# Feed-forward tiles in groups of eight and six, a written plan of shares, and single homes for three buffers

## The chip, the cores and the metric

The kernel runs on one core of a Trainium2 chip. The core has five engines with queues of their own: TensorE (PE in the profile; its weight loads are listed as PEld), VectorE (DVE), ScalarE (ACT), GpSimd (POOL) and SyncE (SP), which here does nothing but start transfers. They work at the same time and wait for each other by semaphores. The metric is the time of one execution on the device in microseconds; the kernel before takes 1460.91 us (median of three runs, 1458.57 to 1462.61).

## The reference

One transformer-like block over 2048 tokens of width 512, all in float32:

```python
xn = layernorm(x)
q, k, v = split(xn @ wqkv)                 # 32 heads of 16
o = softmax(q @ k.T * 16 ** -0.5) @ v      # per head, over all 2048 keys
s = o @ wo
f = (silu(xn @ w_gate) * (xn @ w_up)) @ w_down   # inner width 1792
out = x + s * silu(f)
```

## The kernel before

**Products.** Where float32 accuracy is wanted at the fast matmul form, an operand is split into a rounded part and a rest (`hi`, `lo`), and a product is three: hi·hi, lo·hi, hi·lo. In this text a *product* is one call of `both` (L169 to L171): two matmuls with 64 rows each, one into the bank `bankx` and one into `banky`, which run side by side on PE. The two banks are added by VectorE when a tile is done, and PE can begin the next tile only when both have been read.

**Stages.** The first part (to L749) normalises, turns and projects the tokens to q, k and v, which go to DRAM. Then comes attention, where 88% of the time lies: 32 units (8 groups of 4 heads × 4 blocks of 512 queries), each of 8 steps, together 256 steps (L773 to L812). In a step PE computes the scores of two key tiles of 128 keys, ScalarE takes their exponentials (four of 128×1024 each, L787), and PE multiplies the step before's exponentials with the values (`values`, L358). The scores lie in two buffers in PSUM, so the second key tile's scores wait for the first one's exponentials, and so on from step to step. PE's order in a step: two pairs of score matmuls, the values of the step before, two pairs of score matmuls, and then a *share* of other work.

**The work dealt out.** That other work is a queue of generators (L400 to L403): the feed-forward network for the four blocks of 512 tokens (`ffn`, L180), then the output projection (`project_out`, L317), which for the last block goes over three quarters of the features and for the other three blocks over all. Each `yield` is one product, and `fill(n)` draws n of them. `share` (L423) decides how many a step gets: it divides a tile into equal parts so that the size of a part is near the pace (what is left over the steps that are left). A tile of 24 products so gives 8, 8, 8; one of 21 gives 11 and 10, or 7, 7, 7; one of 12 gives 12, or 6 and 6. In all 2160 products are dealt out over the 256 steps, and 12 are kept for the end.

**Feed-forward.** For each block of tokens the 14 tiles of 128 inner features are taken in two groups of seven (`FG`). First each tile's gate and up product (24 products, `fx` is the block's normalised tokens, `gu` the split weights); at its end ScalarE takes a tanh (`th`, L198), VectorE makes the gated tile `ga` (L199, L200) and splits it into `hh`, and splits the raw w_down rows `wdr` into `wd` (`split_hidden`, L160; L141, L142). Then four output tiles of 128 tokens, each over the group's seven tiles, 21 products; after the first group they are stored in `facc`, after the second added to it as `y` (L218 to L223), and `store_gate` (L173, another tanh in `th`) stores their gate. These calls stand in a list `after` and are made in the next step (`catch_up`). With the last tile of the second group `load_fx` (L144) fetches the next block's `fx`.

**Loads.** All of SyncE's transfers are issued in the order in which the program writes them; one that has to wait for its buffer holds up those behind it. `load_wd(i + 1)` (L186) stands at the start of tile i, with two homes for `wdr`, ahead of `load_gu(i + 2)`. A unit's queries (`load_q`, L803) are fetched one unit ahead, in its first step.

**Output projection.** Each tile of 128 tokens is 12 products (9 for the last block's part). VectorE adds the banks into `y` (L336, L337), GpSimd multiplies by the gate and adds the input (`store_out`, L312) and stores. `ready` counts a block's split inputs, and `fill` stops at a block that isn't ready. In the last unit `load_gate` and `gate_rest` (L344, L352) prepare the last block's rows with eight operations on VectorE (L354, L355). After the last step come the last tile, the last values, and the last block's last quarter (L813 to L853).

Of the kernel before, what the change touches and what calls it, by code (L numbers as in the profile page):

```python
# [9 lines left out]
F32 = mybir.dt.float32  # L10
# [9 lines left out]
P = 128  # L20
S = 2048
D = 512
# [7 lines left out]
KT = S // P  # L30
NG = H // 4
NF = F // P
FG = NF // 2
VW = 4 * (DH + 1)
NROW = 3 * DH + 2
HALF = 64
# [1 line left out]
RING = NB + 1  # L38
DC = D // HALF
LIMIT = 160.0  # L40
EPS = 1e-5
QSLOT = (0, 1, 0)
KSLOT = (0, 0, 1)
# [3 lines left out]
def tile_block(ctx: ExitStack, tc: tile.TileContext, x, wqkv, wo, w_gate, w_up, w_down, out):  # L47
# [84 lines left out]
        gu[i] = (hi, lo)  # L132

    def load_wd(i):
        raw = two.tile([P, D], F32, tag="wdr", name="wdr")
        sp.dma_start(raw, w_down[(i % NF) * P:(i % NF + 1) * P])
        wdr[i] = raw

    def split_wd(i):
        f = i % FG  # L140
        dve.tensor_copy(wd[:, f, 0], wdr[i])  # L141
        dve.tensor_sub(wd[:, f, 1], wdr[i], wd[:, f, 0].bitcast(F32))  # L142

# [16 lines left out]
    def split_hidden():  # L160
        while kept:
            f, i, ga = kept.pop(0)
            dve.tensor_copy(hh[:, f, 0], ga)
            dve.tensor_sub(hh[:, f, 1], ga, hh[:, f, 0].bitcast(F32))
            split_wd(i)

    halves = [slice(h * HALF, (h + 1) * HALF) for h in range(2)]

# [2 lines left out]
            mm(bank, lhs[h], rhs[h], start=start, stop=stop)  # L171

    def store_gate(y, r):  # L173
        th = two.tile([P, D], F32, tag="th", name="th")
        act(th, y, AF.Tanh, scale=0.5)
        dve.scalar_tensor_tensor(y, th, 1.0, y, op0=ALU.add, op1=ALU.mult)
        pool.dma_start(g_d[r:r + P], y)


    def ffn(b):  # L180
        for grp in range(2):
            for f in range(FG):
                i = b * NF + grp * FG + f
                if i + 1 < NB * NF:
                    split_gu(i + 1)
                    load_wd(i + 1)  # L186
                if i + 2 < NB * NF:
                    load_gu(i + 2)
                hi, lo = gu.pop(i)
                n = 0  # L190
                for c in range(DC):
                    for wt, j in ((hi, 0), (hi, 1), (lo, 0)):
                        both(wt[:, c], fx[:, j, c], n == 0, n == 3 * DC - 1)
                        n += 1
                        if n == 3 * DC:
# [8 lines left out]
                            if grp == 1 and f == FG - 1 and b + 1 < NB:  # L204
                                load_fx(b + 1, 0)
                                load_fx(b + 1, 1)
                            elif grp == 1 and f == FG - 1:
                                load_wo(0)
                                load_wo(1)
                        yield 3 * DC - n  # L210
            for t in range(NT):
                n = 0
                for f in range(FG):
                    for a, w in ((0, 0), (0, 1), (1, 0)):
                        both(hh[:, f, a, t * P:(t + 1) * P], wd[:, f, w], n == 0, n == 3 * FG - 1)
                        n += 1
                        if n == 3 * FG and grp == 0:
                            dve.tensor_copy(facc[:, t], bankx)  # L218
                            dve.tensor_add(facc[:, t], banky, facc[:, t])
                        elif n == 3 * FG:  # L220
# [6 lines left out]
                        yield 3 * FG - n  # L227


    wor = {}  # L230

    def load_wo(c):
        wor[c] = two.tile([P, D], F32, tag="wdr", name="wor")
        sp.dma_start(wor[c], wo[c * P:(c + 1) * P])

    def split_wo(c):
# [80 lines left out]
    def project_out(b, n=DT):  # L317
        catch_up()
        for j in range(NT):
            t = b * NT + j  # L320
            i = 0
            for c in range(n):
                for a, w in ((0, 0), (0, 1), (1, 0)):
                    lo, hi = lhs[b, c][a][:, j * P:(j + 1) * P], fx[:, w, c]
                    if t == end:
                        mm(bankx, lo, hi, start=i == 0, stop=i == 3 * n - 1)  # L326
                    else:
                        both(lo, hi, i == 0, i == 3 * n - 1)
                    i += 1
                    if i == 3 * n and n == DT:  # L330
                        y = two.tile([P, D], F32, tag="th", name="y")
                        if t == end:
                            after.append(partial(act, y, bankx, AF.Copy, scale=0.5))
                            after.append(partial(store_out, t, y))
                        else:
                            dve.tensor_scalar(y, bankx, 0.5, None, op0=ALU.mult)  # L336
                            dve.scalar_tensor_tensor(y, banky, 0.5, y, op0=ALU.mult, op1=ALU.add)  # L337
                            store_out(t, y)
                    elif i == 3 * n:
                        dve.tensor_copy(facc[:, j], bankx)  # L340
                        dve.tensor_add(facc[:, j], banky, facc[:, j])
                    yield 3 * n - i

    def load_gate():  # L344
        for i in range(2):
            last.extend((two.tile([P, D], F32, tag="wdr", name="last"), on[i]))
        for t in range(NT):
            r = rows[(NB - 1) * NT + t]
            sp.dma_start(gate[t], g_d[r])
# [47 lines left out]
    u0 = units - NB + 1  # L397


    queue = [[None, ffn(b), NF * 3 * DC + 2 * NT * 3 * FG] for b in range(NB)]  # L400
# [5 lines left out]

    now = -1

    left = 0

    def fill(n):
        nonlocal given, left
        while n > 0 and queue and (queue[0][0] is None or ready[queue[0][0]] == DT):
            left = next(queue[0][1])
            queue[0][2] -= 1
            if not queue[0][2]:
                queue.pop(0)
# [2 lines left out]

    def share():  # L423
        pace = max(1.0, (total - rest - given) / (units * steps - now))
        if left:
            n = left
        elif queue and queue[0][0] is None and len(queue) > NB:
            n = 3 * (DC if ffn_tiles() else FG)
        else:
            n = 3 * DT if queue and queue[0][0] is not None else 3 * (DT - 1)  # L430
        n = -(-n // max(1, round(n / pace)))
        fill(min(n, total - rest - given))


    def ffn_tiles():
        return given % (NF * 3 * (DC + NT)) % (FG * 3 * (DC + NT)) < FG * 3 * DC


    with ExitStack() as pro:
# [89 lines left out]
                dve.tensor_scalar(rt, n1, rt, None, op0=ALU.mult)  # L529

        def norm(t):
            xn[t] = two.tile([P, D], F32, tag="th", name="xn")
            dve.tensor_scalar(xn[t], xin[:, t], mv[:, t, 0:1], rs[:, t:t + 1], op0=ALU.subtract, op1=ALU.mult)  # L533

        def turn_x(b, t, between=None):
# [230 lines left out]

    now = 0
    split_hidden()
    prev = None

    exps = []
    settled = mybir.DependencyInfo(mybir.DependencyClass.Sync, mybir.DependencyReason.DATA)
    for u in range(units):  # L773
        g, b = divmod(u, NB)
        q = qst[u % 2]
        for kp in range(steps):
            now = u * steps + kp
            probs = []
            for i in range(2):
# [9 lines left out]
                        tc.add_manual_dep(exps[-1].ins, exps[-3].ins.name, settled, reason="order of the slots' writes")  # L789
                    probs.append(pr)  # L790
                if now == i == 0:
                    fill(5)
                if i == 0:
                    catch_up()
                if i == 0 and prev:
# [38 lines left out]
    def gated(t):  # L834
        dve.scalar_tensor_tensor(y[t], outs[t], 0.5, gate[t], op0=ALU.mult, op1=ALU.mult)  # L835
# [42 lines left out]
```

## Time and profile before

| | |
|---|---|
| runs | 1460.91 us median, 1458.57 to 1462.61 |
| the profiled execution | 1459.36 us, of which the span from the first to the last instruction is 1457.6 |
| granted clock of PE | 0.998 |
| PE busy | 1441.6 us, 99% of the span |
| ScalarE busy | 1094.5 us, 75%; 992.5 of it the 1024 exponentials, 1023 ns each |
| VectorE, GpSimd busy | 537.7 us (37%), 88.2 us (6%) |
| attention steps | from 168.16 us on; the last begins at 1436.31 |

The first numbers of a timeline line are the start and the length in us, then engine, line, operation, output and inputs; a bracket at the end is how long the engine had stood idle and for whom. Neighbouring instructions of one kind are merged to one line (x4). A line of the stretches view gives the stretch, its length, each engine's busy time, the granted clock, and last the busy share of the DMA engines and GB/s. Matmuls are pipelined and their ends are modelled, so PE is shown busy while it waits inside a merged line; starts tell more than busy time.

### The profile page before, as it was taken

How to read it: one execution, taken by the hardware profiler on the slowest of the kernel's cores; microseconds unless marked ns; L12 is line 12 of the kernel's file. 1: busy time of each engine (PE TensorE's matmuls, PEld its weight loads, DVE VectorE, ACT ScalarE, POOL GpSimd, SP SyncE). 2: the span in 40 equal slices, each digit the busy share in tenths (PEclk: the TensorE clock that was granted, in tenths of full speed). 3: DMA queues.
4: the chain of work that ended last, by engine and by line, in shares of the span. 5: the costliest groups of instructions: out<-in, count | busy, mean ns of one | idle time of the engine just before them, and what ended most of it. 6: DMA issues, size and time to landing. Idle time of an engine off the chain costs nothing.

```text
span 1457.6 us, 26766 instructions
## 1 busy us (share of the span) xinstructions
PE 1441.6 (99%) x11237; PEld 806.6 (55%) x11237; DVE 537.7 (37%) x905; ACT 1094.5 (75%) x1219; POOL 88.2 (6%) x105
## 2 busy tenths in 40 slices
PE   9999999999999999999999999999999999999997
PEld 7777655555555555555555555555555555555544
DVE  6543343124333432234233422343243314334535
ACT  4433588788878887888788878887888778887774
POOL 4100200000000000000000000000000000000234
PEclk9999999999999999999999999999999999999999
DMA  8889652033273331143715311437135202423252
GB/s 267 272 284 287 168 121 58 15 86 88 67 172 84 92 78 34 39 110 72 171 36 120 87 24 34 105 86 171 56 76 130 56 12 46 105 63 128 91 188 73
DMA packets 129556, 154.92 MB, mean 106 GB/s; under 512 B 12700, under 2 KB 79260, under 8 KB 128404
## 3 DMA queue, kind: packets, MB, share of 16 engines
q1 hardware_dynamic: 123940, 130.38, 36.0%
q0 software_dynamic: 5200, 22.22, 4.0%
q8 instruction: 91, 1.49, 0.4%
q10 hardware_dynamic: 288, 0.52, 0.1%
q14 instruction: 37, 0.30, 0.1%
HBM read 111.13 MB, written 41.94 MB: 105 GB/s over the span
## 4 chain that ended last, share of the span: by engine, by line
PE 95%; ACT 2%; DVE 1%; DMA 1%; issue 0%; DVEq 0%; ACTq 0%
PE acc L364 32%; PE bankx L171 29%; PE score L785 20%; PE ps L561 6%; PE banky L171 4%; PE ps L563 3%; ACT pr L787 1%; DMA q_d<-parts 1%; PE acc L538 0%; DVE facc L354 0%; PE bankx L326 0%; DMA facc<-in_A_x_dram 0%; DVE y L835 0%; DVE xn L533 0%; DVE y L838 0%
## 5 line engine op out<-in xcount | busy, mean ns | idle before, releaser
L787 ACT ACTIVATE pr<-score 128x1024 f32<-128x1024 f32 x1024 | 992.5, 1023 | 237.7 <-PE score L785 235.0
L364 PE MATMUL acc<-pr,vst 128*17 128x512 f32 x4096 | 489.2, 595 | 0.0
L785 PE MATMUL score<-qst,kst 50*128 50x512 f32 x2048 | 360.1, 424 | 2.9 <-ACT pr L787 2.0
L785 PEld LDWEIGHTS score<-qst,kst 50*128 50x128 f32 x2048 | 177.8, 184 | 273.2 <-ACT pr L787 236.7
L171 PE MATMUL bankx<-fx,guh 64*128 64x512 f32 x896 | 288.4, 392 | 0.0
L171 PE MATMUL banky<-fx,guh 64*128 64x512 f32 x896 | 288.3, 391 | 0.0
L364 PEld LDWEIGHTS acc<-pr,vst 128*17 128x17 f32 x4096 | 93.9, 96 | 235.4 <-issue 234.6
L199 DVE SCALAR_TENSOR_TENSOR ga<-th,bankx 128x512 f32<-128x512 f32 x56 | 38.5, 687 | 464.1 <-ACT th L198 464.1
L171 PEld LDWEIGHTS bankx<-fx,guh 64*128 64x128 f32 x896 | 165.8, 185 | 32.7 <-issue 0.4
L171 PE MATMUL bankx<-fx,gul 64*128 64x512 f32 x448 | 175.4, 391 | 0.0
L171 PE MATMUL banky<-fx,gul 64*128 64x512 f32 x448 | 175.3, 391 | 0.0
L171 PEld LDWEIGHTS banky<-fx,guh 64*128 64x128 f32 x896 | 165.7, 185 | 4.1
L171 PE MATMUL bankx<-wd,hh 64*128 64x512 f32 x672 | 165.8, 389 | 0.0
L171 PE MATMUL banky<-wd,hh 64*128 64x512 f32 x672 | 165.7, 388 | 0.0
L171 PEld LDWEIGHTS bankx<-wd,hh 64*128 64x128 f32 x672 | 124.0, 184 | 24.9
L171 PEld LDWEIGHTS banky<-wd,hh 64*128 64x128 f32 x672 | 124.0, 184 | 2.1
L171 PEld LDWEIGHTS bankx<-fx,gul 64*128 64x128 f32 x448 | 82.8, 185 | 17.5
L171 PEld LDWEIGHTS banky<-fx,gul 64*128 64x128 f32 x448 | 82.8, 185 | 1.8
L561 PE MATMUL ps<-xt,wh 128*128 128x512 f32 x256 | 80.9, 397 | 0.0
L131 DVE TENSOR_TENSOR gul<-gur,guh 128x1024 fp32r<-128x1024 f32 x56 | 68.6, 1226 | 2.1
L218 DVE COPY facc<-bankx 128x512 f32<-128x512 f32 x16 | 11.1, 691 | 131.1 <-PE banky L171 103.9
L600 ACT CAST parts<-ps 128x512 fp32r<-128x512 f32 x32 | 18.7, 585 | 52.0 <-PE ps L561 24.4
(146 smaller groups left out, 1042.7 us busy)
## 6 DMA issues: line engine op xcount, KB each, us to landing
fx<-xt_d SPq DMA_DIRECT2D x32, 512.0 KB
gur<-in_B_w_gate_dram SPq DMA_DIRECT2D x56, 256.0 KB
gur<-in_B_w_up_dram SPq DMA_DIRECT2D x56, 256.0 KB
wdr<-in_B_w_down_dram SPq DMA_DIRECT2D x56, 256.0 KB
kst<-k_d SPq DMA_DIRECT2D x192, 64.0 KB
qst<-q_d SPq DMA_DIRECT2D x192, 64.0 KB
xt_d<-xt POOLq DMA_DIRECT2D x8, 1024.0 KB, 8.0
q_d<-parts SPq DMA_DIRECT2D x16, 512.0 KB
```

Of the source, the lines that this page charges most:

```text
L131: dve.tensor_sub(lo, raw, hi.bitcast(F32))
L171: mm(bank, lhs[h], rhs[h], start=start, stop=stop)
L199: dve.scalar_tensor_tensor(ga, th, 1.0, bankx, op0=ALU.add, op1=ALU.mult)
L218: dve.tensor_copy(facc[:, t], bankx)
L364: mm(a[h * 32:h * 32 + DH + 1], v[:, kt % CT, h * (DH + 1):(h + 1) * (DH + 1)], probs[2 * i + h // 2][:, h % 2], start=kt == 0, stop=kt == ...
L561: mm(ps, w, a[:, c], start=n == 0, stop=n == 3 * DT - 1)
L563: mm(ps, a[:, c, tokens], w, start=n == 0, stop=n == 3 * DT - 1)
L600: nc.scalar.copy(parts[:, 0], ps)
L785: mm(score[j][:, h], k[r, j, kc * P:(kc + 1) * P], q[r, j], start=True, stop=True)
L787: exps.append(act(pr, score[j], AF.Exp, scale=0.25))
```

## The change

The 14 tiles of a block are taken as eight and six. An output tile of a group has 24 or 18 products for 21; their sum over a block is the same. `share` no longer works out its part: `plan` writes all 256 shares in a list before the first step. Gate tiles go as 8, 8, 8, tiles of the six-group as 9, 9, those of the eight-group as 8, 8, 8 or as 12, 12 (two parts for nine of 16, spread evenly by `HALVED`), the last block's projection as one share of 9 a tile, and the other projection tiles by `OUT_PARTS` as 12 or as 6, 6. Tile 1, of which 15 and 9 products were drawn in two steps, now has three steps of 8, five of them drawn early in step 0 as before.

`hh` and `wd` have eight places each for seven. Room for them comes from buffers that had two homes and have one: `wdr` (w_down rows, and the rows of `wo` and one row of `x` later), `th` (both tanhs, and the projection's `y`), and the pool `late` of the normalisation. `load_wd` is issued in a tile's first third for the tile itself, no longer a tile ahead; `load_wo` one quarter ahead and not two. The normalised tokens of the first part move to the tag `ga`, the last block's third row of `x` goes to `on[2]`, and the tail's rows lie in homes of the exponentials.

```diff
-FG = NF // 2
+GROUPS = (slice(0, 8), slice(8, NF))
+FG = 8
...
+FIRST = 5
+HALVED = 9
+OUT_PARTS = (2, 2, 1, 1, 1, 1, 1, 2, 1, 2, 2)
...
     def load_wd(i):
-        raw = two.tile([P, D], F32, tag="wdr", name="wdr")
+        raw = one.tile([P, D], F32, tag="wdr", name="wdr")
...
     def store_gate(y, r):
-        th = two.tile([P, D], F32, tag="th", name="th")
+        th = one.tile([P, D], F32, tag="th", name="th")
...
-        for grp in range(2):
-            for f in range(FG):
-                i = b * NF + grp * FG + f
+        for grp, part in enumerate(GROUPS):
+            nf = part.stop - part.start
+            for f in range(nf):
+                i = b * NF + part.start + f
                 if i + 1 < NB * NF:
                     split_gu(i + 1)
-                    load_wd(i + 1)
...
                         n += 1
+                        if n == DC and i:
+                            load_wd(i)
                         if n == 3 * DC:
-                            th = two.tile([P, TB], F32, tag="th", name="th")
+                            th = one.tile([P, TB], F32, tag="th", name="th")
...
     def next_out(t):
         split_wo(t)
-        if t + 2 < DT:
-            load_wo(t + 2)
+        if t + 1 < DT:
+            load_wo(t + 1)
...
-                        y = two.tile([P, D], F32, tag="th", name="y")
+                        y = one.tile([P, D], F32, tag="th", name="y")
...
     def load_gate():
-        for i in range(2):
-            last.extend((two.tile([P, D], F32, tag="wdr", name="last"), on[i]))
+        last.extend(on[:3] + [one.tile([P, D], F32, tag="wdr", name="last")])
...
+    shares = []
+
+    def plan():
+        def tile_of(n, parts):
+            shares.extend([n // parts] * parts)
+
+        halved = 0
+        for i in range(2 * NB):
+            nf = GROUPS[i % 2].stop - GROUPS[i % 2].start
+            for _ in range(nf - (i == 0)):
+                tile_of(3 * DC, 3)
+            for t in range(NT):
+                if nf == FG:
+                    halved += HALVED
+                    tile_of(3 * nf, 3 - halved // (NB * NT))
+                    halved %= NB * NT
+                else:
+                    tile_of(3 * nf, 2)
+        for _ in range(NT):
+            tile_of(3 * (DT - 1), 1)
+        for parts in OUT_PARTS:
+            tile_of(3 * DT, parts)
+        shares[0] -= FIRST
+
+    def blocked():
+        return not queue or queue[0][0] is not None and ready[queue[0][0]] < DT
+
     def share():
-        pace = max(1.0, (total - rest - given) / (units * steps - now))
...
-        fill(min(n, total - rest - given))
+        if not blocked() and shares:
+            fill(shares.pop(0))
...
         def norm(t):
-            xn[t] = two.tile([P, D], F32, tag="th", name="xn")
+            xn[t] = two.tile([P, D], F32, tag="ga", name="xn")
...
-    late = ctx.enter_context(tc.tile_pool(name="late", bufs=2))
+    late = ctx.enter_context(tc.tile_pool(name="late", bufs=1))
...
+    spare, *y = [ppool.tile([P, 2, TB], F32, tag="pr", name="y") for _ in range(3)]
+    y = [i[:, n] for i in y for n in range(2)]
     turned = []
     for n in range(2):
         normalise(units - 1, n * half, (n + 1) * half, partial(low, 0) if n else None)
-        turned.append(late.tile([P, TB], F32, tag="o2", name="o2"))
+        turned.append(spare[:, n])
...
-    y = [where.tile([P, D], F32, tag=tag, name="y") for where, tag in ((two, "ga"), (late, "o1")) * 2]
```

More of the change, by code (lines that the diff above doesn't have):

```diff
@@ L203, in ffn @@
                                 split_hidden()
-                            if grp == 1 and f == FG - 1 and b + 1 < NB:
+                            if grp == 1 and f == nf - 1 and b + 1 < NB:
                                 load_fx(b + 1, 0)
                                 load_fx(b + 1, 1)
-                            elif grp == 1 and f == FG - 1:
+                            elif grp == 1 and f == nf - 1:
                                 load_wo(0)
-                                load_wo(1)
                         yield 3 * DC - n
@@ L212, in ffn @@
                 n = 0
-                for f in range(FG):
+                for f in range(nf):
                     for a, w in ((0, 0), (0, 1), (1, 0)):
-                        both(hh[:, f, a, t * P:(t + 1) * P], wd[:, f, w], n == 0, n == 3 * FG - 1)
+                        both(hh[:, f, a, t * P:(t + 1) * P], wd[:, f, w], n == 0, n == 3 * nf - 1)
                         n += 1
-                        if n == 3 * FG and grp == 0:
+                        if n == 3 * nf and grp == 0:
                             dve.tensor_copy(facc[:, t], bankx)
                             dve.tensor_add(facc[:, t], banky, facc[:, t])
-                        elif n == 3 * FG:
+                        elif n == 3 * nf:
                             y = two.tile([P, D], F32, tag="ga", name="y")
@@ L226, in ffn @@
                                 after.append(partial(next_out, t))
-                        yield 3 * FG - n
+                        yield 3 * nf - n
     wor = {}
     def load_wo(c):
-        wor[c] = two.tile([P, D], F32, tag="wdr", name="wor")
+        wor[c] = one.tile([P, D], F32, tag="wdr", name="wor")
         sp.dma_start(wor[c], wo[c * P:(c + 1) * P])
@@ L397, in tile_block @@
     u0 = units - NB + 1
-    queue = [[None, ffn(b), NF * 3 * DC + 2 * NT * 3 * FG] for b in range(NB)]
+    queue = [[None, ffn(b), NF * 3 * (DC + NT)] for b in range(NB)]
     queue += [[None, project_out(NB - 1, DT - 1), NT * 3 * (DT - 1)]]
@@ L407, in tile_block @@
     now = -1
-    left = 0
     def fill(n):
-        nonlocal given, left
-        while n > 0 and queue and (queue[0][0] is None or ready[queue[0][0]] == DT):
-            left = next(queue[0][1])
+        nonlocal given
+        while n > 0 and not blocked():
+            next(queue[0][1])
             queue[0][2] -= 1
@@ L419, in fill @@
             given += 1
-    def share():
-        pace = max(1.0, (total - rest - given) / (units * steps - now))
[L425 to L431, printed above, removed]
-        fill(min(n, total - rest - given))
-    def ffn_tiles():
-        return given % (NF * 3 * (DC + NT)) % (FG * 3 * (DC + NT)) < FG * 3 * DC
+    shares = []
[21 more added lines that the diff above has]
+        return not queue or queue[0][0] is not None and ready[queue[0][0]] < DT
+    def share():
+        if not blocked() and shares:
+            fill(shares.pop(0))
     with ExitStack() as pro:
@@ L768, in tile_block @@
     split_hidden()
+    plan()
     prev = None
@@ L791, in tile_block @@
                 if now == i == 0:
-                    fill(5)
+                    fill(FIRST)
                 if i == 0:
```

5 lines of the change are left out of this document (2 added, 3 removed).

## The prediction

> **What bounds the kernel now.** First the chain that ended last, on the profile's page (share of the span by engine, then by line):
>
> ```profile
> PE 95%; ACT 2%; DVE 1%; DMA 1%; issue 0%; DVEq 0%; ACTq 0%
> PE acc L364 32%; PE bankx L171 29%; PE score L785 20%; PE ps L561 6%; PE banky L171 4%; PE ps L563 3%; ACT pr L787 1%; DMA q_d<-parts 1%; PE acc L538 0%; DVE facc L354 0%; PE bankx L326 0%; DMA facc<-in_A_x_dram 0%; DVE y L835 0%; DVE xn L533 0%; DVE y L838 0%
> ```
>
> TensorE (PE) carries it, and the number of its instructions is the same after the change. So the only question is where PE stands waiting inside the 256 attention steps. The chain doesn't show that; the waits do (engine, line, waited for: us in total, times, longest):
>
> ```profile
> PEld score L785 <- ACT pr L787: 236.7, 317, 0.9
> SPq L136 <- DVE wd L142: 427.9, 45, 35.8
> ```
>
> A score weight load waits for ScalarE's exponentials 317 times. Mostly other matmuls run meanwhile, so I looked at how long steps are. In the timeline of PE every step starts with the four score matmuls of its first key tile (start us, length, what), so the difference of two such starts is a step. First the end of a group of feed-forward tiles, then the output projection:
>
> ```profile
> 421.40 0.63 PE L785 MATMUL score<-qst,kst 50*128 50x512 f32 x4
> 426.89 0.63 PE L785 MATMUL score<-qst,kst 50*128 50x512 f32 x4
> 432.15 0.65 PE L785 MATMUL score<-qst,kst 50*128 50x512 f32 x4
> 436.74 0.87 PE L785 MATMUL score<-qst,kst 50*128 50x512 f32 x4
> 441.55 0.86 PE L785 MATMUL score<-qst,kst 50*128 50x512 f32 x4
> 446.36 0.86 PE L785 MATMUL score<-qst,kst 50*128 50x512 f32 x4
> ```
> ```profile
> 1358.84 0.62 PE L785 MATMUL score<-qst,kst 50*128 50x512 f32 x4
> 1364.59 0.64 PE L785 MATMUL score<-qst,kst 50*128 50x512 f32 x4
> 1368.97 0.39 PE L785 MATMUL score<-qst,kst 50*128 50x512 f32 x2
> 1369.54 0.50 PE L785 MATMUL score<-qst,kst 50*128 50x512 f32 x2 [0.18 <-ACT pr L787]
> 1373.77 0.39 PE L785 MATMUL score<-qst,kst 50*128 50x512 f32 x2
> ```
>
> The six rows of the first list bound steps of 11, 10, 7, 7 and 7 products: 5.49, 5.26, 4.59, 4.81, 4.81. The next, of 8, takes 5.06, although an 8 in a row of eights takes 4.84. A product in a run is 0.2325 us, so a 7 should take 4.61 each time. The first does; then the score group is longer (0.87 for 0.65), because its second half waits for ScalarE. So ScalarE sets a floor of 4.80 a step, and what a short step can't pay is paid by the next. The second list bounds 12, 6 and 6 (the third and fourth row are one group that the wait splits): 5.75, 4.38, 4.80, then 12 again at 6.20. A six loses 4.80 − 4.37 = 0.43, a seven 0.2, and steps from eight up are paid at 4.84 (8), 5.07 (9), 5.26 (10), 5.50 (11), 5.75 (12).
>
> **The change, part by part.** All sums are against the profiled execution, 1459.36 us, which is 1.55 below the median of 1460.91.
>
> *Shares, feed-forward output tiles.* Before, each of eight groups takes 399.82 to 446.36 = 46.54 us for its nine output steps (11, 10 three times, 7, 7, 7), and 0.22 in the next eight: 46.76, times 8 = 374.1. After, from the plan: the four groups of six give 32 nines; in the four groups of eight, 9 of 16 tiles go as two twelves (18) and 7 as three eights (21). 32 × 5.07 + 18 × 5.74 + 21 × 4.84 = 162.2 + 103.3 + 101.6 = 367.1, and some 0.05 for the tanh in the first step of each group (in the 46.54 it is in the first 11, 5.56 for 5.50): 367.5. A twelve is 5.73 (11 plus a product) to 5.75 (the row). That is −6.6, in 71 steps for 72.
>
> *The step given back.* Tile 1 now takes 8, 8, 8 in steps 0 to 2, where it took 15 and 9 in two (168.16 to 178.65, 10.5 us). Step 0 has no value matmuls to cover the exponentials, which run without a gap from 168.94 for 3.77 us. With 3 products for 10 behind its second scores, PE waits for the fourth exponential (172.71), and the value matmuls start at about 173.1 for 174.16: 7 products, 1.63 us, less work for 1.06 us less time, so 0.57 lost. Then 5.44 and 4.84: about 14.1 in all, +3.6; between +3.0, a step with no loss, and +3.7.
>
> *The first projection step* (9 products, 6.15 for 5.07) waits for VectorE's chain of output row, gate and two splits (L223, L176, L238, L257). Of the 1.08, 0.2 is the seven's debt, counted above. Without it PE is at the seventh product 0.2 sooner and the splits are not: +0.1, between 0 and 0.4.
>
> *Output projection.* Ten sixes and six twelves before and after, in another order. Before, sixes stand in pairs behind a twelve; after, 6,6,6,6, five twelves, 6,6, a twelve, 6,6,6,6. Each six still costs 0.43, whatever its neighbours, but the last has no score behind it that waits (−0.4). And VectorE's gate work, which was in the way once, is now placed better:
>
> ```profile
> 1426.27 0.68 DVE L354 SCALAR_TENSOR_TENSOR facc<-facc,wd 128x512 f32<-128x512 f32 x1
> 1428.92 0.68 DVE L336 TENSOR_SCALAR y<-bankx 128x512 f32<-128x512 f32 x1
> ```
> ```profile
> 1429.66 0.50 PE L171 MATMUL bankx<-fx,hh 64*128 64x512 f32 x1 [0.45 <-DVE y L336]
> ```
>
> Between 1421.55 and 1428.92 VectorE does eight operations on the last rows (L354, L355); a twelve ended at 1426.09, its banks came free late, and that six took 5.63 for 4.37. After, the twelve ends before these 7.4 us begin and the next tile ends 9.2 us later (6, 6), so the wait goes. It was part of what the sixes wait for anyway. Step 240 to the last product takes 1358.84 to 1442.5 = 83.7 now; after, 4.37 + 3 × 4.80 + 6.20 + 4 × 5.75 + 4.37 + 4.80 + 6.20 + 4.37 + 3 × 4.80 = 82.1. So −1.6, between −0.4 and −2.7. The tail behind it (15 us) is unchanged: last values now start 1.4 us sooner behind the scores, but the last exponentials end 2.5 us behind those scores (602.34 to 604.83 in a step of eight) and are needed only by the second half of the values, 0.58 + 1.40 + 0.92 = 2.9 behind.
>
> *Single homes.* For `wdr`, SyncE today waits at the load for the split of the tile before (the second wait above; 389.14 + 0.69 ends the split, 389.86 is the issue). The new load waits for that same split, behind the gate and up weights for ahead of them, and has nothing else behind it earlier than today. Transfers issued from 389.86 had left the DMA engines by 395 (share 0.82, then 0.00); the split that needs it comes one tile, 14.5 us, after the split that released it. So 0; if uncovered, up to 5.2 us for each of 55 tiles. `th`: the next tanh is two steps away at least: 0. As `y` in the projection it is read by GpSimd until 4.45 us behind a tile's last product (1442.55 to 1447.00; 5.1 where VectorE was busiest), and the five twelves come 5.75 apart: 0; uncovered, VectorE's write may still slip 1.5 us before PE at its first product, 3.0 behind, notices. `late`, the tail's rows in the `pr` slots, and the fourth row in `on`, whose load waits for VectorE some 5 us, 13 us ahead of use: 0.
>
> The rule that speaks against this: "Double-buffer for performance" (the Trainium skill, Trainium Kernel Development and Optimization, Best Practices). By it the lost second home of `wdr` would end the overlap and the sum would be 1459.36 − 4.5 + 55 × 5.2 = 1741; the rows give 14.5 us of room for 5.2, so I go by them and keep the rule as a rival.
>
> Sum: −6.6 + 3.6 + 0.1 − 1.6 = −4.5, so 1454.9 against this profile and 1456.4 against the median. Ends: −2.5 to −6.8.
>
> **The rivals.**
> (a) *Twelves aren't clean.* The row of 5.75 follows a nine; a twelve behind sixes costs 6.20. If eights leave a debt too (4.84 lies only 0.04 over the floor), 18 twelves at 0.25 more take the gain away: 1460.9. Against it: elevens beside eights and tens stay at 5.50.
> (b) *Slower: the queries queue behind the reload of `fx`.* With the new counts the reloads fall at the ends of steps 48 and 168, the first step of a unit, so the next unit's queries stand right behind them and are due seven nines later, 35.5 us. Before, the same queue took from 399.31 until the DMA share fell to 0.00 at 430:
>
> ```profile
> 399.31 5.15 SPq L148 DMA_DIRECT2D fx<-xt_d x8
> 404.56 13.98 SPq L96 DMA_DIRECT2D qst<-q_d  x6
> 430.00:432.00 2.00, 2.00 (x22) 1.66 (x20) 0.00 (x0) 1.78 (x2) 0.00 (x0) 1.00 0.00 0
> ```
>
> That is 30.7 us, 4.8 to spare. Beyond 35.5 each us is paid twice; it eats the gain from 37.8 and is slower by 0.3% from 40: say 42, 1469.
> (c) *A load in a single home is on the path*: if the loads took over 14.5 us, each us more in the few tiles whose split ends a group, 8 of them, would be PE's: at 16 us +12, 1468. Against it: 5.2 measured. This is what the Trainium skill's rule, named above, warns of.
> (d) *More gain*: step 0 loses nothing, the projection gains its 2.7 and eights become 0.02 cheaper with no sevens near them (186 of them, 3.7): −10.5, 1450.
> (e) *The plan isn't followed*: a blocked step takes no share, and its products run alone at the end. One twelve moved so is 2.8 − 0.95 = +1.9. Readiness comes at steps 238, 240 and 248, ahead of 240, 246 and 251: very unlikely.
>
> **How the numbers follow.** Forecast 0.60, (a) and (e) 0.10, (b) 0.08, (c) 0.06, (d) 0.16. A measurement tells 0.3%, 4.4 us, from no change, and the forecast lies on that edge: 0.32 of its 0.60 beyond it, 0.28 within. Faster 0.32 + 0.16 = 0.48; same 0.28 + 0.10 = 0.38; slower 0.14. Time 1456.4; its own range 1454.1 to 1458.4. The full range, 1452 to 1463, leaves out the far end of (d) and most of (b) and (c).
>
> **What would show it.** No seven left; nines at 5.07, twelves at 5.75 wherever no six stands before; three first steps of about 3.8, 5.4, 4.8; no wait of PE for L336; the wait of the score load for ScalarE smaller in feed-forward output steps. Wrong if eights are above 4.86, if a bank waits for GpSimd through `y`, or if scores wait for a transfer at steps 56 or 176.

## The result and the profile after

The kernel after takes 1453.62 us (median of seven runs, 1451.71 to 1455.91) against 1460.91 of before (seven runs); the ratio is 0.9956, 95% interval 0.9943 to 0.9968. It is faster, by 0.44%. The profiled executions are 1451.71 and 1459.36 us, their spans 1449.9 and 1457.6.

The chain that ended last, on the page of the kernel after, still runs almost wholly over PE's matmuls (L367, L174 and L803 are what L364, L171 and L785 were before). It could be followed back only to 165.7 us, where attention begins, which is why its shares add up to 89%:

```profile
PE 86%; ACT 2%; DVE 1%; issue 0%; DVEq 0%; ACTq 0%
PE acc L367 32%; PE bankx L174 30%; PE score L803 20%; PE banky L174 3%; ACT pr L805 2%; PE bankx L330 0%; DVE y L854 0%; DVE y L857 0%; DVE rl L839 0%; PE score L863 0%; DVE fx L242 0%; DVE y L179 0%; DVEq L893 0%; ACT th L178 0%; DVE fx L241 0%
```

So the comparison is by steps, as before: the difference between the starts of two steps' first score matmuls. With the products counted between them, each stretch of the two profiled executions can be set side by side (us; the last column is the prediction's term):

| stretch | before | after | difference | predicted |
|---|---|---|---|---|
| before the first step | 168.16 | 166.50 | −1.66 | not in the sum |
| tile 1 (two steps, three steps) | 10.49 | 14.13 | +3.64 | +3.6 |
| rest of the feed-forward steps, to step 235 | 1158.84 | 1150.70 | −8.14 | −6.6 |
| first projection steps, 236 to 239 | 21.35 | 21.32 | −0.04 | +0.1 |
| step 240 to the end | 98.71 | 97.29 | −1.43 | −1.6 |
| span | 1457.55 | 1449.93 | −7.62 | −4.5 |

In the timeline of PE the three starts below bound two nines of an output tile of a six-group, 5.10 (with the tanh of the gate tile before) and 5.04:

```profile
406.97 0.63 PE L803 MATMUL score<-qst,kst 50*128 50x512 f32 x4
...
412.07 0.63 PE L803 MATMUL score<-qst,kst 50*128 50x512 f32 x4
...
417.11 0.63 PE L803 MATMUL score<-qst,kst 50*128 50x512 f32 x4
```

There is no longer a score group of 0.87 in such a place. The sixes of the projection, now in a row, still have it, cut in two by the wait: 4.36, 4.82, 4.80:

```profile
1352.65 0.64 PE L803 MATMUL score<-qst,kst 50*128 50x512 f32 x4
...
1357.01 0.40 PE L803 MATMUL score<-qst,kst 50*128 50x512 f32 x2
1357.58 0.51 PE L803 MATMUL score<-qst,kst 50*128 50x512 f32 x2 [0.18 <-ACT pr L805]
...
1361.83 0.39 PE L803 MATMUL score<-qst,kst 50*128 50x512 f32 x2
```

Around step 0 PE waits twice (the two groups with a bracket naming ScalarE). The first wait, for the second exponential, was there before the change too; the second, for the fourth exponential, is new, since three products behind the second scores are too few. Step 1 begins at 170.32, and step 0's values come at 171.5, 5.0 us behind step 0's start:

```profile
166.50 0.93 PE L803 MATMUL score<-qst,kst 50*128 50x512 f32 x4 [1.61 <-PEq L734]
168.36 0.50 PE L803 MATMUL score<-qst,kst 50*128 50x512 f32 x2
169.27 0.50 PE L803 MATMUL score<-qst,kst 50*128 50x512 f32 x2 [0.41 <-ACT pr L805]
170.32 0.40 PE L803 MATMUL score<-qst,kst 50*128 50x512 f32 x2
171.11 0.50 PE L803 MATMUL score<-qst,kst 50*128 50x512 f32 x2 [0.38 <-ACT pr L805]
```

The waits of the kernel after (us in total, times, longest): the score loads' wait for ScalarE has fallen by 18 of 317 times, SyncE's for the split before a `wdr` load is about what it was (427.9, 45 times before), and VectorE waited once for a `wdr` transfer, which it never did before:

```profile
PEld score L803 <- ACT pr L805: 229.2, 299, 0.9
SPq L140 <- DVE wd L145: 402.9, 46, 14.1
DVE wd L144 <- DMA wdr<-in_B_w_down_dram: 2.2, 1, 2.2
```

VectorE's eight operations for the last rows end at 1425.20, and the next tile's banks are read at once, 0.3 us later; no matmul waits for L340 any more:

```profile
1424.51 0.69 DVE L358 TENSOR_TENSOR facc<-facc,last 128x512 f32<-128x512 f32 x1
1425.53 0.69 DVE L340 TENSOR_SCALAR y<-bankx 128x512 f32<-128x512 f32 x1 [0.33 <-PE banky L174]
```

### The profile page after: what moved, and what is told of

Same layout as the page of the kernel before. It is cut to its first block, busy times and chain, and to the rows that moved or that the text cites. A ratio compares the mean times of both kernels' runs of the same rounds, so it can differ in the third digit from the quotient of the medians.

```text
span 1449.9 us, 26818 instructions
## 1 busy us (share of the span) xinstructions
PE 1433.2 (99%) x11237; PEld 804.1 (55%) x11237; DVE 539.9 (37%) x905; ACT 1094.4 (75%) x1219; POOL 89.9 (6%) x105
## 4 chain that ended last, share of the span: by engine, by line
PE 86%; ACT 2%; DVE 1%; issue 0%; DVEq 0%; ACTq 0%
PE acc L367 32%; PE bankx L174 30%; PE score L803 20%; PE banky L174 3%; ACT pr L805 2%; PE bankx L330 0%; DVE y L854 0%; DVE y L857 0%; DVE rl L839 0%; PE score L863 0%; DVE fx L242 0%; DVE y L179 0%; DVEq L893 0%; ACT th L178 0%; DVE fx L241 0%
## 5 line engine op out<-in xcount | busy, mean ns | idle before, releaser
L367 PE MATMUL acc<-pr,vst 128*17 128x512 f32 x4096 | 489.2, 595 | 0.0
L803 PE MATMUL score<-qst,kst 50*128 50x512 f32 x2048 | 354.8, 422 | 4.0 <-ACT pr L805 2.4
L803 PEld LDWEIGHTS score<-qst,kst 50*128 50x128 f32 x2048 | 177.3, 184 | 268.9 <-ACT pr L805 229.2
L174 PE MATMUL bankx<-fx,guh 64*128 64x512 f32 x896 | 288.6, 392 | 0.0
L174 PE MATMUL banky<-fx,guh 64*128 64x512 f32 x896 | 288.5, 392 | 0.0
L367 PEld LDWEIGHTS acc<-pr,vst 128*17 128x17 f32 x4096 | 93.9, 96 | 235.9 <-issue 235.0
L174 PEld LDWEIGHTS bankx<-fx,guh 64*128 64x128 f32 x896 | 165.7, 185 | 34.3 <-issue 0.4
L174 PE MATMUL banky<-fx,gul 64*128 64x512 f32 x448 | 175.4, 392 | 0.0
L174 PE MATMUL bankx<-fx,gul 64*128 64x512 f32 x448 | 175.3, 391 | 0.0
L174 PEld LDWEIGHTS banky<-fx,guh 64*128 64x128 f32 x896 | 165.7, 185 | 2.7
L174 PE MATMUL banky<-wd,hh 64*128 64x512 f32 x672 | 165.4, 388 | 0.0
L174 PE MATMUL bankx<-wd,hh 64*128 64x512 f32 x672 | 165.4, 388 | 0.0
L174 PEld LDWEIGHTS bankx<-wd,hh 64*128 64x128 f32 x672 | 124.0, 184 | 25.6
L174 PEld LDWEIGHTS banky<-wd,hh 64*128 64x128 f32 x672 | 124.0, 184 | 1.4
L174 PEld LDWEIGHTS bankx<-fx,gul 64*128 64x128 f32 x448 | 82.9, 185 | 17.9
L174 PEld LDWEIGHTS banky<-fx,gul 64*128 64x128 f32 x448 | 82.8, 185 | 1.4
L390 POOL DMA_DIRECT2D o_d<-o x12 | 7.5, 623 | 825.6 <-DVE o L388 825.6
```

The source lines that it names most:

```text
L367: mm(a[h * 32:h * 32 + DH + 1], v[:, kt % CT, h * (DH + 1):(h + 1) * (DH + 1)], probs[2 * i + h // 2][:, h % 2], start=kt == 0, stop=kt == ...
L390: (pool if g < NG - 1 else sp).dma_start(o_d[g // 2, b], o2)
L803: mm(score[j][:, h], k[r, j, kc * P:(kc + 1) * P], q[r, j], start=True, stop=True)
```

## The experiments

Times of stretches below are from each kernel's own profiled execution, from the start of the first step on, since the time up to there differs from run to run for a reason of its own (last section). Before, the stretch from step 0 to the end is 1289.40; after, 1283.43. A kernel for which no median is given ran once.

### The buffers alone

```diff
 # in the kernel before; groups of seven and share() stay
-        raw = two.tile([P, D], F32, tag="wdr", name="wdr")
+        raw = one.tile([P, D], F32, tag="wdr", name="wdr")
...
-                    load_wd(i + 1)
...
+                        if n == DC and i:
+                            load_wd(i)
...
-        th = two.tile([P, D], F32, tag="th", name="th")
+        th = one.tile([P, D], F32, tag="th", name="th")
...
-    late = ctx.enter_context(tc.tile_pool(name="late", bufs=2))
+    late = ctx.enter_context(tc.tile_pool(name="late", bufs=1))
...
```

> The kernel before with the buffers of the change alone: one home for the raw w_down rows, the tanh and the normalisation, the weights' load for the tile itself in its first third, wo one quarter ahead, the tail's rows in the exponentials' homes; groups of seven and the shares as before. Theory (the plan of shares carries the gain): no change, 1460.9 within 0.2%, the 236 feed-forward steps 1169.3 us as before, sevens again 4.80 from the second on, the projection from its step 240 to the end 98.7. Rival 1 (buffers and the loads' order carry it): 3 us or more faster with the old shares. Rival 2 (a single home exposes its load): a wait of VectorE for the weights' transfer in most of 55 tiles, and 1465 or more.

Measured: 1458.85 us (median of ten), ratio to before 0.9990, interval 0.9981 to 1.0000. The feed-forward steps take 1169.30 (before 1169.33), step 240 to the end 98.68 (98.71). The sevens stand where they stood, 436.57 to 441.39 to 446.20:

```profile
436.57 0.87 PE L784 MATMUL score<-qst,kst 50*128 50x512 f32 x4
...
441.39 0.86 PE L784 MATMUL score<-qst,kst 50*128 50x512 f32 x4
...
446.20 0.86 PE L784 MATMUL score<-qst,kst 50*128 50x512 f32 x4
```

VectorE waits for a weights' transfer in two tiles, the first two of attention (tile 1 at 186.6 us, tile 2 at 197.4):

```profile
DVE wd L141 <- DMA wdr<-in_B_w_down_dram: 5.7, 2, 4.7
```

It costs PE nothing: from step 0 to the end it is 1289.33 for 1289.40. So the buffers are neither the gain nor a loss; their worth is the room for the eighth place. (The ratio's interval just reaches 1, so a gain of a tenth of a per cent outside these steps isn't excluded.) The reverse, groups of eight with the old number of homes, was not run.

### The projection's order

```diff
-OUT_PARTS = (2, 2, 1, 1, 1, 1, 1, 2, 1, 2, 2)
+OUT_PARTS = (1, 2, 1, 2, 1, 2, 1, 2, 1, 2, 1)
```

> The kernel after with the projection's shares in the order of before: a twelve and two sixes in turn. Theory: steps 0 to 239 as after (1164.8 and 21.3); from step 240 on 1.4 more than after (97.3), because the last six has a score behind it again (0.43) and VectorE's eight operations for the last rows stand in front of a bank again (a six of 5.6). Rival (only the number of sixes counts, ten each): 97.3 within 0.3.

Measured: feed-forward 1164.90, steps 236 to 239 21.32, step 240 to the end 98.72, which is 1.43 more than after; the six behind the last rows' operations takes 5.64 again, and the last six has a score group behind it again. So the projection's 1.4 us are the order's, as the theory has it.

### More sixes

```diff
-HALVED = 9
+HALVED = 16
...
-                    tile_of(3 * nf, 2)
+                    tile_of(3 * nf, 3 if i < 2 or i == 3 and t < 3 else 2)
```

> The kernel after with all 16 output tiles of the eight-groups as two twelves (7 tiles less in three parts) and 7 of the 16 tiles of the six-groups as three sixes instead of two nines: the same products in the same 256 steps, 21 sixes more. Theory (a step under eight products costs 4.80 whatever it holds): 21 x 0.43 = 9.0 us more in steps 0 to 235 than after (1164.8), so 1173.8; the sixes 4.80 but the first of each row, twelves 6.2 behind a six. Rival (PE's work and the number of steps alone count): 1164.8 within 1.

Measured: feed-forward 1173.89, 9.06 more than after, for 9.0 expected. The same 2160 products in the same 256 steps, cut otherwise, cost 9 us: what decides is how much falls under the floor. In the row of sixes that begins at step 47 the first takes 4.41, and from the third on they take 4.79 to 4.83. Here the third and the fourth, between the starts 411.99, 416.79 and 421.59:

```profile
411.99 0.40 PE L803 MATMUL score<-qst,kst 50*128 50x512 f32 x2
412.57 0.50 PE L803 MATMUL score<-qst,kst 50*128 50x512 f32 x2 [0.18 <-ACT pr L805]
...
416.79 0.40 PE L803 MATMUL score<-qst,kst 50*128 50x512 f32 x2
...
421.59 0.40 PE L803 MATMUL score<-qst,kst 50*128 50x512 f32 x2
```

### Tile 1 in two steps, and more products early

```diff
-HALVED = 9
+HALVED = 8
...
-        shares[0] -= FIRST
+        shares[:3] = [15 - FIRST, 9]
```

> The kernel after with tile 1 in two steps of 15 and 9 as before, and the step so won given to one more output tile of an eight-group in three parts (8 of 16 in two parts). Theory: steps 0 and 1 take 10.5 (for three steps of 14.1), and steps 0 to 235 0.6 us less than after, 1164.2, since PE no longer waits for step 0's fourth exponential with too little work. Rival (the step given back costs only its own length): 1164.8 within 0.2.

Measured: steps 0 and 1 take 5.46 + 5.05 = 10.51, the feed-forward steps 1164.26: 0.57 less than after, as expected. The same with eight products between the two key tiles of step 0:

```diff
-FIRST = 5
+FIRST = 8
```

> The kernel after with tile 1 in two steps of 15 and 9, of which 8 instead of 5 are drawn between the two key tiles of step 0, and 8 of 16 tiles of the eight-groups in two parts. Theory: three products more cover PE's wait for the second exponential, so step 0 takes 4.7 where it takes 5.46 with 5 drawn early. Rival (the four exponentials set step 0's length whatever PE does between): 5.46 within 0.1.

Step 0 takes 4.74, and no matmul waits inside it:

```profile
166.25 0.93 PE L803 MATMUL score<-qst,kst 50*128 50x512 f32 x4 [1.25 <-ACT vt L632]
168.68 0.85 PE L803 MATMUL score<-qst,kst 50*128 50x512 f32 x4
170.99 0.82 PE L803 MATMUL score<-qst,kst 50*128 50x512 f32 x4
```

Of the 0.72, 0.20 comes back: the score group at 170.99 is 0.82 long and step 1 takes 5.25 for 5.05. The two steps together are 0.52 shorter than with five early; the feed-forward steps as a whole, 1163.46, are 0.80 shorter, of which 0.28 lies scattered over the other 234.

### The splits' order

```diff
     def next_out(t):
+        if t:
+            split_o(lhs[NB - 1, t - 1], plain[t - 1])
         split_wo(t)
...
-        else:
-            split_o(lhs[NB - 1, t - 1], plain[t - 1])
```

> The kernel after with the order of two splits changed in the step after an output tile of the last group: first the part that the projection multiplies next, then the quarter of wo that it doesn't need yet. Theory (the first projection step waits for VectorE's chain): step 236 falls from 6.15 by 0.9, to 5.2 or 5.3, all else as after. Rival (the wait is for the gate's tanh, or for the transfer of the part): 6.15 within 0.1.

Step 236 takes 5.08 (for 6.15), 1332.27 to 1337.34, all else is as after within 0.2. The line of the kernel after that this removes stands first, the new starts below it:

```profile
1336.41 0.50 PE L174 MATMUL bankx<-fx,part 64*128 64x512 f32 x1 [0.55 <-DVE part L261]
```
```profile
1332.27 0.63 PE L803 MATMUL score<-qst,kst 50*128 50x512 f32 x4
...
1337.34 0.63 PE L803 MATMUL score<-qst,kst 50*128 50x512 f32 x4
```

So the wait was for two operations on `wo` that stood ahead on VectorE, 1.1 us long, and not for the tanh or a transfer.

### No sixes, and everything together

```diff
-HALVED = 9
+HALVED = 4
-OUT_PARTS = (2, 2, 1, 1, 1, 1, 1, 2, 1, 2, 2)
+OUT_PARTS = (1,) * 11
...
-            if now == (units - 1) * steps + 3:
-                gate_rest()
+            if now >= (units - 1) * steps + 4:
+                gate_rest(((0,), (1,), (2, 3), ())[now - (units - 1) * steps - 4])
```

> The kernel after with every projection tile as one twelve (11 steps for 16) and the five steps so won given to output tiles of the eight-groups, of which 4 of 16 instead of 9 now go as two twelves; the eight operations for the last rows go one row a step over the last unit. Theory: nine debts of 0.43 us go, and from step 0 to the end it is 3.9 us shorter than after (1283.4), 1279.5. Rival 1 (a step of six costs what it holds, only products and steps count): 1283.4 within 0.3. Rival 2 (one home for y in eleven twelves in a row makes VectorE, and then PE, wait for GpSimd): twelves over 6.0 us, and at least 1283.

Measured: 1284.32 from step 0 to the end, 0.9 more than after and not 3.9 less. The ten twelves that the dealt steps show are clean (5.76 to 5.78), so rival 2 doesn't hold. But steps 241 and 242, nines, take 8.49 and 7.41, together 4.7 more than the first two projection steps of after (6.15 and 5.05); without these 4.7 it would be 1279.6, as the theory has it, and not rival 1's 1283.4. With all changes together (the diffs above, with `HALVED = 3`, `FIRST = 8`):

> All of these together: projection tiles as twelves, 3 of 16 tiles of the eight-groups as two twelves, tile 1 in two steps with 8 products drawn early, the splits' order changed, the last rows' operations spread. Theory: the gains add, 3.9 + 0.6 + 0.7 + 0.9 = 6.1 us less than after from step 0 to the end (1283.4), 1277.3, and 0.991 of the time before. Rival (they overlap, since a debt removed is only shifted to the next wait): 1280 or more, 0.993.

1451.09 us (median of five), ratio 0.9939, interval 0.9925 to 0.9953; 1280.89 from step 0 to the end for 1277.3: the rival's number came. Its reason did not, for again two steps are long, 7.04 and 6.70, together 3.6 more than two nines, and the rest is as the theory has it. VectorE's timeline in the first of them:

```profile
1346.04 0.70 DVE L374 STREAM_TRANSPOSE o<-acc 128x512 f32<-128x512 f32 x1
...
1348.73 0.69 DVE L262 TENSOR_TENSOR wd<-o,wd 128x512 fp32r<-128x512 f32 x1
1349.34 0.68 DVE L179 SCALAR_TENSOR_TENSOR y<-th,y 128x512 f32<-128x512 f32 x1
1349.94 0.42 DVE L261 CAST part<-pair 128x512 fp32r<-128x512 f32 x1
```
```profile
1350.42 0.50 PE L174 MATMUL bankx<-fx,part 64*128 64x512 f32 x1 [1.44 <-DVE part L261]
```

The five steps more had moved the feed-forward network's end to step 240, in which VectorE also normalises unit 29: 3.4 us (1346.04 to 1349.42) in front of the gate and of the part that the projection needs. PE waits, and for the 3.4 us from 1352.30 the granted clock is 0.50, which makes the next nine 1.6 longer:

```profile
1352.30:1355.60 3.30, 3.30 (x18) 0.63 (x12) 1.14 (x2) 1.56 (x2) 0.00 (x0) 0.50 0.71 266
```

So I let the network end one step sooner, and the last dealt tile go as two sixes:

```diff
-HALVED = 3
+HALVED = 4
-OUT_PARTS = (1,) * 11
+OUT_PARTS = (1,) * 10 + (2,)
```

> As the version with everything together, but the feed-forward network ends one step earlier (step 239; 4 of 16 eight-group tiles as two twelves) and the last dealt projection tile goes as two sixes in the last two steps, so that the first projection step no longer falls together with the normalisation of a unit on VectorE. Theory: the first projection steps take 5.05 each (for 7.0 and 6.7), and from step 0 to the end it takes 1277.5 (after 1283.4, less 3.4 for eight debts, 0.6, 0.8 and 1.1). Rival (the two long steps came from the transfers, which are later by their place in the program): again a step over 6, and 1280 or more.

1446.36 us (median of four), ratio to before 0.9906, interval 0.9889 to 0.9922: faster than before, and by the ratios (0.9956, 0.9943 to 0.9968) faster than after, beside which it did not run. From step 0 to the end 1277.68, for 1277.5. The first projection step is 5.11:

```profile
1346.65 0.64 PE L803 MATMUL score<-qst,kst 50*128 50x512 f32 x4
...
1351.76 0.63 PE L803 MATMUL score<-qst,kst 50*128 50x512 f32 x4
```

The gains add, once the new coincidence is out of the way. That it was the coincidence and not the transfers is shown by VectorE's order above and by this run together; the place in the program moved by one step only.

### What the floor is made of

```diff
 # in the kernel before; a scratch tile more[0] is zeroed ahead of the steps
+                    if i == 1 and j == 1:
+                        act(more[1], more[0], AF.Exp)
                     probs.append(pr)
```

> The kernel before with one more, useless operation on ScalarE in each step, an exponential of 128x16 behind the four, about 0.2 us by the rows of small operations. Theory (the floor of 4.80 is ScalarE's chain of four exponentials, and eights lie 0.04 over it): the floor rises to about 5.0; sevens and sixes from the second on 5.0, eights rise from 4.84 to 5.0, nines stay near 5.07, tens, elevens and twelves as before; about 30 us more in all. Rival (the floor is PE's own order of weight loads and score buffers): every step as before, within 0.05.

My theory fell: the operation takes 0.22 us on ScalarE in every step, and sevens (4.80 from the second on), eights (4.84) and all others from step 2 on are as before. (Steps 0 and 1 are 2.0 us longer, since the zeroing of the scratch tile stands behind VectorE's first splits.) ScalarE's timeline shows why: the operation ends where ScalarE would have waited for the next scores, and the wait is shorter by it:

```profile
605.83 0.22 ACT L793 ACTIVATE more<-more 128x16 f32<-128x16 f32 x1
606.35 1.94 ACT L789 ACTIVATE pr<-score 128x1024 f32<-128x1024 f32 x2 [0.31 <-PE score L787]
```

Four exponentials are 3.88 us, so ScalarE is free for almost 1 us of a 4.80 step. What comes back to itself every 4.80 us is a loop through both engines. Between two sevens of the kernel before: scores of the second key tile at 439.37, third and fourth exponential 439.91 to 441.85, the second half of the next scores, which needs the fourth exponential's buffer, to 442.34, the values to 444.18, and there the next step's scores of the second key tile begin: 0.54 + 1.94 + 0.49 + 1.84 = 4.81. The share of products stands beside the exponentials in this loop, and the first two exponentials beside the values. So the operation has to lie between the third and the fourth:

```diff
-                    if i == 1 and j == 1:
+                    if i == 1 and j == 0:
```

> The kernel before with the same useless operation (0.21 us) between the third and the fourth exponential of each step, no longer behind the fourth. New theory (the floor is a loop: scores of the second key tile, third and fourth exponential, second half of the next step's first scores, values, scores of the second key tile: 0.54 + 1.94 + 0.49 + 1.84 = 4.81): now the operation lies in the loop, the floor rises to 5.0, sevens and sixes from the second on take 5.0, eights 5.0, nines 5.07, longer steps as before, some 30 us more in all. Rival (a floor that isn't ScalarE's at all): every step as before, within 0.05.

Now eights are 4.91, all three of a gate tile alike, sevens and sixes from the second on 4.90, and nines, tens and elevens as before. The starts of two eights, and ScalarE in the loop:

```profile
600.48 0.95 PE L787 MATMUL score<-qst,kst 50*128 50x512 f32 x4
...
605.37 0.96 PE L787 MATMUL score<-qst,kst 50*128 50x512 f32 x4
```
```profile
448.74 1.03 ACT L789 ACTIVATE pr<-score 128x1024 f32<-128x1024 f32 x1 [0.90 <-PE score L787]
449.66 0.20 ACT L793 ACTIVATE more<-more 128x16 f32<-128x16 f32 x1
449.77 2.98 ACT L789 ACTIVATE pr<-score 128x1024 f32<-128x1024 f32 x3
```

The place was right and the size half of what I expected: the fourth exponential starts 0.10 later, not 0.21, because the operations overlap (449.66 + 0.20 is behind 449.77). The score groups of eights are 0.95 long, for 0.64 before: they have come under the floor. The feed-forward steps take 1188.04; 6.6 of the 18.7 more stand in step 1 alone (11.67 for 5.05), where PE waits 3.81 for the scratch tile and the clock is at half from 176.0 to 182.8, and say nothing of the floor. The rest, some 12 us, is what 0.07 to 0.10 in 162 eights and the shorter steps come to.

## Why the prediction was right, point by point

*The time.* 1456.4 was forecast and 1453.62 measured, inside 1452 to 1463; the forecast's own range, 1454.1 to 1458.4, was missed by 0.5 at its lower end. Faster by over 0.3% had the largest chance, and so it came; but the sum itself, −4.5, lay at the edge of what can be told from no change, and that the gain stands clear of it is owed in part to what the forecast missed. Of the 2.8 between forecast and measurement, the profiles show two parts.

*A term left out.* The stretch before attention was taken as unchanged. In the profiled execution of before it held 3.4 us at half clock, in that of after none. Half of 3.4 is 1.7, about the 1.66 that it took longer; as starts without such a stretch spread from 165.9 to 167.4, how much of the 1.66 is the clock's isn't shown. It isn't the change's: the kernel with the buffers alone has it again (167.86), and so have the three kernels with the change's plan that ran beside it (167.99 to 170.51). How much of it is left between the medians of seven runs stays open.

*The feed-forward shares* were mis-sized: −6.6 forecast, −8.14 measured. The nine was priced by the projection's 5.07 and is 5.04 in the feed-forward network (32 of them, 1.0), twelves are 5.73 and the output tiles' eights 4.82 for 4.84 (0.3 and 0.5 in all). The projection's steps are 0.03 longer than the network's for the same number of products (twelves 5.77 for 5.73) because the products themselves start 0.233 us apart in its twelves and 0.229 in the network's; why they do stays open. That a six costs 0.43 is borne out by the 21 sixes, 9.06 for 9.0; the seven's 0.2 rests on the rows alone. The sum's ends (−2.5, −6.8) and rival (d)'s −10.5 lie some 0.4 to 0.6 outside what the bounds given for the single terms add up to: some play in the feed-forward shares must be in them that isn't stated, and this is the term that was off.

*The reason of the floor* was wrong: not ScalarE's four exponentials, but the loop of 4.81 through PE and ScalarE, as the useless operation shows (nothing behind the fourth exponential, 0.10 between the third and the fourth). The prices were read off rows and so didn't depend on it. Rival (a), that eights leave a debt, didn't come: eights lie 0.04 over the floor, and twelves behind them are 5.71 to 5.75.

*The step given back* (+3.64 for +3.6) and its reason, too few products in step 0, are shown by the two runs with tile 1 in two steps: with the old 15 and 9 the 0.57 come back, and with eight products early another 0.52 that the kernel before lost too. *The first projection step* is 6.15 before and after: VectorE's splits set it, as the run with their order changed shows, and the seven's debt only hid in it. *The projection* (−1.43 for −1.6) went by its two reasons; the run with the old order gives both back.

*Single homes*: 0 forecast, and 0 measured from step 0 to the end with the buffers alone. That every `wdr` load has 14.5 us of room was too much said: tile 1's, at the start of attention, was issued at 181.32, and VectorE stood idle for it for 2.2 us, until 186.37, with nobody behind it on PE. The rule of the Trainium skill (Trainium Kernel Development and Optimization, Best Practices) is to double-buffer for performance. Here a second home was worth nothing to PE, where 14.5 us of room stood against 5.2.

*Rival (b)*, queries behind the reload of `fx`, didn't come: the reload was issued at 406.46, the DMA engines' share is 0.00 from 434, and the next unit starts at 442.29 without a wait; 28 us fit into 36. *Rival (c)* didn't come either. *Rival (d)* named the right side, but none of its three reasons came: step 0 does lose its 0.57, the projection gained 1.43 and not 2.7, and the eights of gate tiles with no seven before them take 4.85 before and after. *Rival (e)*: the plan was followed in all 256 steps.

## What to carry to other kernels

When one engine is busy 99% of the time, measure the length of a loop's turn against the work dealt to it: where the curve goes flat, short turns are paid for work that they don't hold, and the same work cut into turns that stay over the flat part is faster. Find what the flat part is made of by a useless operation put at two places: only what lies in the loop moves it. And before work is moved by a few turns, look what else falls into the turn where it will end; a coincidence on an engine that is 37% busy cost in one run here more than the move brought (4.7 us for 3.9).

## What the runs showed of the hardware

PE's granted clock falls to half for stretches of 3.41 us (once or twice on end), mostly in the first 170 us, and at other places in other runs. In the stretches view, the column before the DMA share is the granted clock; before, and with the projection's old order, where it came twice:

```profile
163.60:166.90 3.30, 3.30 (x10) 2.42 (x8) 0.00 (x0) 1.20 (x2) 1.15 (x3) 0.50 0.72 176
```
```profile
138.50:141.80 3.30, 3.30 (x9) 2.56 (x9) 0.69 (x1) 0.76 (x2) 0.00 (x0) 0.51 0.72 266
165.90:169.10 3.20, 3.20 (x9) 2.52 (x8) 0.00 (x0) 1.31 (x2) 1.27 (x3) 0.50 0.70 173
```

Without any before it, attention starts at 165.9 to 167.4 (four profiles); with one, at 167.3 to 169.2 (seven); with two or three, at 170.5 and 171.2. So a part of the few microseconds by which executions of one kernel differ may lie here: of the seven of the kernel after, the fastest has a mean granted clock of 0.998, the three slowest (1455.50 to 1455.91) 0.995 and 0.996, and the three between 0.997. Stretches from step 0 on therefore compare better than whole times. Inside attention, apart from the end, when PE has finished, it came only where PE had stood idle: after 1.44 us of waiting in the run with everything together (one stretch), around 2.50 us in the run without sixes (6.8 us on end), around the 3.81 us for the scratch tile (6.8 us), and after 1.99 us in front of step 0 in the other kernel with the scratch tile. No step that waited 0.8 or less at a time was followed by one. But idle time of that length need not bring it: in five profiles PE stood idle for 1.25 to 1.69 us in front of step 0 (1.61 in the kernel after), and none followed. The Trainium skill (TensorE: Matmul & The Clock Gate, Part 1) gives a window of 3413 ns over which the clock is decided, which the length agrees with, and puts the slow state after at least one idle window; here it came once with PE idle for 1.44 us at most at a time, so a wait much shorter than the window can be enough, and what else decides isn't shown.
